# Attention, expert layer and MLP on one core: block means transposed behind the scores, first gated blocks and gate sums moved, operand fetches issued by ScalarE, short output blocks emptied in twos, one output piece moved, start-up loads and filler matmuls rearranged

## The chip, the core and the metric

One core of a Trainium2 chip runs the whole program: TensorE (PE, with its weight loads as PEld), VectorE (DVE), ScalarE (ACT), GpSimd (POOL) and SyncE (SP, which issues the DMAs). The metric is the device time of one launch in microseconds; the median of the runs counts.

## What is computed

```python
def reference(**kwargs):
    attn_out = _attn_ref(q, k, v)              # 2 x 8 heads, 768 tokens, 64 wide
    x = np.ascontiguousarray(attn_out.transpose(0, 2, 1, 3)).reshape(B * S, H * D)
    x = _moe_ref(x=x, **moe_kwargs)            # 1536 x 512, 4 experts of 1024
    return _moe2_ref(x=x, **moe2_kwargs)       # 512 -> 2048 -> 512
...
    k_sum = k.reshape(B, H, nb, block, D).max(axis=3)      # blocks of 32 keys
    v_sum = v.reshape(B, H, nb, block, D).mean(axis=3)
    scores_all = np.concatenate([scores_l_m, scores_s], axis=-1)   # 16-wide band, and 24 blocks
    a = np.exp(scores_all - np.max(scores_all, axis=-1, keepdims=True))
    a = a / (np.sum(a, axis=-1, keepdims=True) + 1e-09)
    return np.matmul(a, np.concatenate([v, v_sum], axis=2))
...
    p = domain_probs / (domain_probs.sum(-1, keepdims=True) + 1e-09)
    for e in range(E):
        out += p[:, e:e + 1] * (np.maximum(x @ w1[e], 0.0) @ w2[e])
...
    h = x @ w_in
    return (h * (1.0 / (1.0 + np.exp(-1.702 * h)))) @ w_out
```

## The kernel before

All matmuls of the two dense layers are done as three products of a high and a low part (hi·hi, hi·lo, lo·hi). A low part is always the original minus the high part, so each operand costs a ScalarE cast and a subtraction on VectorE or GpSimd. The order of the work on every engine is written out by hand: Python closures are called in the order in which the engines get their instructions, and each engine works through its own list in order.

**Attention** runs in 24 groups (batch, pair of heads, four windows of 64 queries) and 27 slots. Slot i (`att_a`, `att_b`) does the scores of group i (PE, then VectorE adds the mask, L239, and takes the maximum), the exponentials on ScalarE (L251), the normalisation of group i-1 on GpSimd (`normalise`, L261), the transposes of group i-2 (L269) and the products with v of group i-3 (`values`, L282). The 24 block means of v come in through `means`: `sums` on VectorE, one PE transpose per pair of heads (L218), a ScalarE scaling (tile `vm`) and, for every group, a GpSimd copy into that group's v tile (`vw` or `v_home`, L220). `values` needs this copy. The weights of expert 0 are split in between (`middle`, L167 and L168). `spin` issues filler matmuls on the identity (L943) in the first slots.

**Expert 0, first tokens** runs between the slots: `early` and `first` compute hidden blocks (L387; PSUM banks 0 to 3 for the first four blocks), `hidden` applies ReLU and gate (`gated`, L331, the VectorE operation that empties the bank) and splits the result (L401, L337), and `second` computes the output blocks into the same banks 0 to 3 (L418). The gates are made by `gates` from the loaded probabilities, written to DRAM (L319) and loaded again spread over all partitions (`load_p`).

**Pairs.** From 150 us on, 44 pairs of hidden tiles follow, each as seven products (L664, PSUM banks 6 and 7, called X and Y) of one step of a Strassen-like scheme. ScalarE copies three of them out of Y (m1, L724; r, L734; q, L739), VectorE adds X to such a copy (L716), then come activation, cast (L711) and low part (L337; on GpSimd for two of the four quarters in a pair whose operands are fetched). Between the products stand pieces of the second layer of the pair before (`fill`): 8 pieces of six matmuls in an expert pair (L782; a main block of 512 tokens in its own bank and a side block of 256 tokens, two side blocks to a bank), 12 pieces of three matmuls in the last layer (L807). `product(y, j, 0)` and `product(x, j, 1)` open a pair. The first piece of a pair uses the high and low parts of both quarters of hidden tile f=1 of the pair before.

The first-layer operands `wA` are computed once and parked in DRAM (`keep`); for 20 pairs they are fetched back (`again`, 1.8 MB into one of two `wA` buffers) by SP. In the pairs in between GpSimd and VectorE also convert the last layer's weights (tile `arena`; SP loads them, L592, and stores them, L631). At the end of the expert layer `of_expert` empties the banks: main blocks and side blocks apart, for each of the four d (L792 and L799 for the side blocks).

```python
        product(y, j, 0, (0, 0), True)
        ...
        nc.scalar.copy(m1, cy)
        lead()
        more()
        product(x, j, 1, (1, 0), True)
        g = total_of(cx, m1)
        ...
        fill(1)
        product(y, j, 4, 1, False)
        nc.scalar.copy(r, cy)
        ...
        fill(3)
        product(y, j, 5, 2, False)
```

## Time and profile before

| | |
|---|---|
| median of 3 runs | 865.87 us (865.20 to 867.35) |
| the profiled execution | 866.81 us, of which the span of the profile is 865.0 us |
| mean granted TensorE clock | 0.993 |
| PE busy | 830.1 us, 96% of the span |
| VectorE, GpSimd, ScalarE busy | 602.0, 479.6, 397.1 us |

The time of an execution is the span and 1.8 us around it. The span has three stages: attention with expert 0 (0 to 150 us), expert pairs (150 to 600 us), pairs of the last layer (600 to 865 us). In the rows further down, an entry in brackets such as "[2.40 <-DMA wA<-kept]" is the idle time of that engine just before the row and what ended it; "x6" is the number of instructions merged into the row.

### The profile page before, as it was taken

The numbers are of one execution on the slowest core, as the hardware profiler recorded it, in microseconds if no ns is written. First come the engines' busy times: TensorE is split into PE (matmuls) and PEld (weight loads), VectorE is DVE, ScalarE is ACT, GpSimd is POOL, SyncE is SP. The second block draws the span as 40 slices with busy tenths as digits, with TensorE's granted clock in tenths as the row PEclk, the third lists the DMA queues.
The fourth block names the chain that finished last, engine by engine and source line by source line (L and its number), as shares of the span: only waits on it lengthen the run. The fifth ranks groups of instructions, "written<-read, shape, count | busy, mean of one in ns | idle before, by whom it ended". The sixth has DMA issues, their size and how long they took to land.

```text
span 865.0 us, 13668 instructions
## 1 busy us (share of the span) xinstructions
PE 830.1 (96%) x5068; PEld 748.7 (87%) x5068; DVE 602.0 (70%) x899; ACT 397.1 (46%) x914; POOL 479.6 (55%) x416
## 2 busy tenths in 40 slices
PE   6978999999999999989999999999899999999998
PEld 5866778899999989889989998999788998998896
DVE  7677538879999884688788688897788753432332
ACT  4766742535444444233333334446556453434442
POOL 6657435656667674265564657867478642323221
PEclk9899999999999999999999999999999999999999
DMA  9853412366767536386776874223534627653422
GB/s 284 255 174 87 138 38 103 117 249 244 266 218 264 207 149 259 114 314 231 277 252 251 287 276 143 77 73 110 183 134 169 232 110 280 207 193 112 150 93 74
DMA packets 48371, 159.93 MB, mean 185 GB/s; under 512 B 5424, under 2 KB 8752, under 8 KB 43184
## 3 DMA queue, kind: packets, MB, share of 16 engines
q1 hardware_dynamic: 48304, 159.06, 53.3%
q8 instruction: 40, 0.66, 0.3%
q14 instruction: 27, 0.22, 0.1%
HBM read 110.78 MB, written 48.26 MB: 184 GB/s over the span
## 4 chain that ended last, share of the span: by engine, by line
PE 72%; DVE 14%; DMA 6%; issue 4%; ACT 2%; POOL 2%; SPq 0%; DVEq 0%; POOLq 0%; ACTq 0%
PE o L782 19%; PE Y L664 17%; PE o L807 13%; PE X L664 5%; PE h L387 3%; DVE S L547 3%; PE o L418 2%; DMA wA<-kept 2%; DVE hid L337 2%; PE sc L231 2%; DVE g L716 2%; PE xo L282 1%; DVE x L452 1%; DMA q<-kq 1%; DVE g L709 1%
## 5 line engine op out<-in xcount | busy, mean ns | idle before, releaser
L782 PE MATMUL o<-hid,wB 128*128 128x512 f32 x1344 | 261.3, 336 | 3.5 <-DVE y L799 2.3
L782 PEld LDWEIGHTS o<-hid,wB 128*128 128x128 f32 x1344 | 214.6, 188 | 25.4 <-DVE y L799 3.0
L576 POOL TENSOR_TENSOR wB<-rawB,wB 128x512 fp32r<-128x512 f32 x88 | 124.9, 1429 | 136.8 <-ACT wB L575 122.0
L807 PE MATMUL o<-wB,hid 128*128 128x512 f32 x576 | 147.8, 393 | 0.0
L711 ACT CAST hid<-g 128x384 fp32r<-128x384 f32 x176 | 90.7, 516 | 117.8 <-DVE g L701 82.4
L337 DVE TENSOR_TENSOR hid<-g,hid 128x384 fp32r<-128x384 f32 (+2 forms) x152 | 129.3, 858 | 19.1 <-ACT hid L711 13.6
L807 PEld LDWEIGHTS o<-wB,hid 128*128 128x128 f32 x576 | 106.9, 188 | 17.0
L552 POOL TENSOR_TENSOR wA<-S,wA 128x512 fp32r<-128x512 f32 x48 | 70.3, 1465 | 45.5 <-ACT wA L551 30.1
L701 DVE SCALAR_TENSOR_TENSOR g<-g,pb 128x384 f32<-128x384 f32 x84 | 83.3, 991 | 2.0
L552 POOL TENSOR_TENSOR wA<-rawA,wA 128x512 fp32r<-128x512 f32 (+1 forms) x48 | 59.7, 1243 | 42.0 <-ACT wA L551 36.4
L664 PE MATMUL Y<-xh,wA 128*128 128x384 f32 x224 | 66.2, 336 | 4.3 <-DMA wA<-kept 2.8
L664 PE MATMUL Y<-xt,wA 128*128 128x384 f32 x336 | 67.5, 335 | 1.7 <-ACT prq L724 1.5
L337 POOL TENSOR_TENSOR hid<-g,hid 128x384 fp32r<-128x384 f32 x40 | 45.6, 1141 | 30.0 <-ACT hid L711 30.0
L724 ACT COPY prq<-Y 128x384 f32<-128x384 f32 x44 | 21.2, 481 | 85.0 <-PE Y L664 68.7
L664 PEld LDWEIGHTS Y<-xt,wA 128*128 128x128 f32 x336 | 56.0, 188 | 4.7 <-ACT prq L724 2.0
L716 DVE TENSOR_TENSOR g<-X,prq 128x384 f32<-128x384 f32 x44 | 24.4, 555 | 43.0 <-PE X L664 40.3
L575 ACT CAST wB<-rawB 128x512 fp32r<-128x512 f32 x88 | 52.5, 619 | 1.4 <-DMA rawB<-wts 1.4
L261 POOL TENSOR_TENSOR s<-s,sm 128x480 f32<-128x480 f32 x24 | 28.3, 1180 | 40.9 <-DVE sm L260 38.5
L708 ACT ACTIVATE sg<-g 128x384 f32<-128x384 f32 x48 | 25.3, 527 | 55.9 <-DVE g L716 55.7
L709 DVE TENSOR_TENSOR g<-g,sg 128x384 f32<-128x384 f32 x48 | 34.2, 713 | 21.5 <-ACT sg L708 19.9
L664 PEld LDWEIGHTS Y<-xh,wA 128*128 128x128 f32 x224 | 41.2, 188 | 7.4 <-DVE arena L605 2.7
L615 POOL TENSOR_SCALAR arena<-arena 128x512 int32<-128x512 int32 x32 | 25.4, 792 | 39.6 <-DVE arena L611 39.6
(451 smaller groups left out, 1633.2 us busy)
## 6 DMA issues: line engine op xcount, KB each, us to landing
kept<-wA SPq DMA_DIRECT2D x20, 1792.0 KB, 6.7
wA<-kept SPq DMA_DIRECT2D x20, 1792.0 KB, 8.7
arena<-w SPq DMA_DIRECT2D x32, 512.0 KB, 4.9
rawB<-wts SPq DMA_DIRECT2D x28, 512.0 KB, 4.0
rawA<-wts SPq DMA_DIRECT2D x16, 512.0 KB, 7.8
w<-arena SPq DMA_DIRECT2D x32, 256.0 KB, 2.5
rawB<-w SPq DMA_DIRECT2D x16, 512.0 KB, 4.3
rawA<-w SPq DMA_DIRECT2D x8, 512.0 KB, 8.0
```

Source lines behind the costliest of these rows:

```text
L261: nc.gpsimd.tensor_tensor(out=s, in0=s, in1=sm.unsqueeze(2).to_broadcast([P, GW, KA]), op=ALU.mult)
L337: engine.tensor_tensor(out=hl, in0=g, in1=hh.bitcast(F32), op=ALU.subtract)
L552: nc.gpsimd.tensor_tensor(out=lo, in0=x, in1=hi.bitcast(F32), op=ALU.subtract)
L575: nc.scalar.copy(hi, rawB[j][:, f])
L576: nc.gpsimd.tensor_tensor(out=lo, in0=rawB[j][:, f], in1=hi.bitcast(F32), op=ALU.subtract)
L664: nc.tensor.matmul(ps[:, 0:HS], ws[w], xs[x][:, k], start=(fresh and k == 0 and m == 0), stop=(k == 1 and m == 2), skip_group_check=True,)
L701: nc.vector.scalar_tensor_tensor(out=g, in0=g, scalar=0.0, in1=pbs[ph, s][:, tok], op0=ALU.max, op1=ALU.mult)
L709: nc.vector.tensor_tensor(out=g, in0=c, in1=sg, op=ALU.mult)
L711: heads.append(lambda: nc.scalar.copy(hh, g))
L716: nc.vector.tensor_tensor(out=g, in0=ps, in1=x, op=ALU.add)
L782: nc.tensor.matmul(o, wB[j][:, w, f, c], tiles[f][:, x, t], start=fr, stop=last, skip_group_check=True,)
L807: nc.tensor.matmul(o, tiles[f][:, x, c], wB[j][:, w, f], start=(new and f == 1 and m == 0), stop=(old and f == 0 and m == 2),)
```

## The change

It has seven parts.

1. `means` is called in `att_a` right after the scores, instead of in `att_b` after the products with v. Its PE transposes (8 in all) go into free columns of the bank that the latest `values` used (bank 7), not into a bank of their own. GpSimd's copy of a slot so stands ahead of its normalisation, split and fold.
2. The gates: the sum over experts becomes two GpSimd additions and a GpSimd add of 1e-9 (`gates_sum`, slot 0), VectorE keeps only the reciprocal, GpSimd multiplies (slot 1 instead of 4); `load_p` moves one slot forward. The probabilities are loaded as SP's 3rd transfer, not its 21st; the q tile of group 4 is the 20th, not the 22nd.
3. `hidden` of blocks 0 to 3 is called about one slot sooner, and its low parts are no longer held back by a queue of their own.
4. The operand fetches `again` are issued by ScalarE, not by SP.
5. The side blocks at the end of an expert stage are emptied two at a time.
6. One second-layer piece (two in the last layer) moves from behind `product(x, j, 1)` to ahead of it; one piece moves from behind `product(y, j, 4)` to ahead of it.
7. `spin` issues 4, 8, 4, 4 filler matmuls in slots 0 to 3 (0, 4, 4, 4 before) and four more behind the transposes of slots 2 and 3. One weight split of slot 3 moves from GpSimd to VectorE. `split_a(0)`, the first pair's operands, is done in eight single steps four and three blocks before the end of expert 0, not in the last three blocks.

```diff
     def means(g):
...
-            ps = bank(5 if b else 4, f"pvs{b}{hp}")
-            nc.tensor.transpose(ps[0:KA, 0:P], vsum[hp % 2], ident)
-            nc.scalar.mul(vms[b, hp][KW:KA], ps[KW:KA, 0:P], 1.0 / BLK)
+            if "ps" not in xo:
+                xo["ps"] = bank(7, "xo")
+            ps = xo["ps"][:, GQ : GQ + P]
+            nc.tensor.transpose(ps[0:KA], vsum[hp % 2], ident)
+            nc.scalar.mul(vms[b, hp][KW:KA], ps[KW:KA], 1.0 / BLK)
...
+    def gates_sum():
+        two, one = ds[:, 0 : NE // 2], ds[:, NE // 2]
+        nc.gpsimd.tensor_tensor(out=two, in0=dp[:, 0 : NE // 2], in1=dp[:, NE // 2 :], op=ALU.add)
+        nc.gpsimd.tensor_tensor(out=one, in0=two[:, 0], in1=two[:, 1], op=ALU.add)
+        nc.gpsimd.tensor_scalar(
+            out=one, in0=one, scalar1=1.0, scalar2=1e-9, op0=ALU.mult, op1=ALU.add
+        )
...
         def again():
             wA[j] = slot("wA", [P, 2, NF - 1, HB], F32R, f"wA{j}", 2)
-            nc.sync.dma_start(out=flat(j), in_=kept[kept_at(j)])
+            nc.scalar.dma_start(out=flat(j), in_=kept[kept_at(j)])
...
         more()
+        fill(1)
         product(x, j, 1, (1, 0), True)
...
-        fill(1)
+        fill(2)
         product(y, j, 4, 1, False)
...
-                    nc.vector.tensor_tensor(
-                        out=y[:, d, 512:S], in0=side, in1=y[:, d, 512:S], op=ALU.add
-                    )
+                    if d % 2:
+                        o = y[:, d - 1 : d + 1, 512:S]
+                        nc.vector.tensor_tensor(out=o, in0=both, in1=o, op=ALU.add)
...
-                    nc.vector.tensor_copy(xf["y1"][:, d, 512:S], side)
+                    if d % 2:
+                        nc.vector.tensor_copy(xf["y1"][:, d - 1 : d + 1, 512:S], both)
...
     def att_a(i):
         if i < NG:
             scores(groups[i])
+        if 2 <= i < NG + 2:
+            means(groups[i - 2])
...
+        spin(SPIN_MORE.get(i, 0))
         if 3 <= i < NG + 3:
             values(groups[i - 3])
-        if 2 <= i < NG + 2:
-            means(groups[i - 2])
...
-        3: [lambda: split(2, A, pool), lambda: split(3, A, dve)],
+        3: [lambda: split(3, A, dve), lambda: split(2, A, dve)],
...
-    SPIN = (0, 4, 4, 4)
+    SPIN = (4, 8, 4, 4)
+    SPIN_MORE = {2: 4, 3: 4}
...
+    for i in range(2):
+        hidden(i)
...
+        if i in (N - 5, N - 4):
+            for _ in range(4):
+                weights.pop(0)()
```

**GpSimd's list in slots 12 and 13.** L220 (L224 after) is the copy of the means into a group's v tile, L261 (L265) the normalisation of a group's score tile s, L168 a weight split, L200 and L181 a fold of k and of v. Before:

```order
L168 TENSOR_TENSOR w0ex_102<-raw_a1_96,w0ex_102 128x512
L220 COPY vw018_659<-vm01_325 24x512
L261 TENSOR_TENSOR s038_860<-s038_860,sm038_893 128x480
L200 COPY kw120_947<-ks12_899 128x4x24
L181 TENSOR_TENSOR vT10_736<-vT10_736 128x24x16
L220 COPY vw028_734<-vm02_398 24x512
L261 TENSOR_TENSOR s100_940<-s100_940,sm100_969 128x480
L200 COPY kw130_1016<-ks13_975 128x4x24
L168 TENSOR_TENSOR w0ex_102<-raw_b_97,w0ex_102 128x512
L181 TENSOR_TENSOR vT11_833<-vT11_833 128x24x16
L220 COPY vw038_831<-vm03_469 24x512
```

The same place in the changed kernel:

```order
L224 COPY vw028_757<-vm02_380 24x512
L265 TENSOR_TENSOR s038_874<-s038_874,sm038_907 128x480
L200 COPY kw120_962<-ks12_913 128x4x24
L181 TENSOR_TENSOR vT10_759<-vT10_759 128x24x16
L224 COPY vw038_845<-vm03_449 24x512
L265 TENSOR_TENSOR s100_954<-s100_954,sm100_983 128x480
L200 COPY kw130_1031<-ks13_989 128x4x24
L168 TENSOR_TENSOR w0ex_102<-raw_b_97,w0ex_102 128x512
L181 TENSOR_TENSOR vT11_847<-vT11_847 128x24x16
```

The copy of group 038 now stands ahead of the normalisation of s100, and so ahead of that slot's fold, split and second fold, which before were all queued in front of it.

**VectorE's list in slots 8 and 9.** g is a hidden block after ReLU and gate, and h2 and h3 are the PSUM banks 2 and 3 that it empties; L239 (L243 after) adds the mask to the scores of a group. Before:

```order
L337 TENSOR_TENSOR hid0_663<-g_664,hid0_663 128x256
L239 SCALAR_TENSOR_TENSOR s018_693<-sc018_684,mask_73 128x480
L244 TENSOR_REDUCE nm018_695<-s018_693 128x4
L259 TENSOR_SCALAR sm008_650<-sm008_650 128x4
L260 RECIPROCAL sm008_650<-sm008_650 128x4
L199 COPY kw038_700<-k03_127 128x4x96
L168 TENSOR_TENSOR w0A1_99<-raw_b_97,w0A1_99 128x512
L337 TENSOR_TENSOR hid0_663<-g_667,hid0_663 128x256
L297 TENSOR_TENSOR xl0_187<-xo024_713,xh0_186 128x256
L187 TENSOR_REDUCE ks10_730<-k10_545 128x24
L331 SCALAR_TENSOR_TENSOR g_741<-h2_373,pb00_480 128x256
L331 SCALAR_TENSOR_TENSOR g_744<-h3_377,pb00_480 128x256
```

The same place in the changed kernel:

```order
L349 TENSOR_TENSOR hid0_625<-g_626,hid0_625 128x256
L349 TENSOR_TENSOR hid0_625<-g_629,hid0_625 128x256
L301 TENSOR_TENSOR xl0_192<-xo014_663,xh0_191 128x256
L343 SCALAR_TENSOR_TENSOR g_687<-h2_399,pb00_430 128x256
L343 SCALAR_TENSOR_TENSOR g_690<-h3_403,pb00_430 128x256
L243 SCALAR_TENSOR_TENSOR s018_715<-sc018_706,mask_73 128x480
L248 TENSOR_REDUCE nm018_717<-s018_715 128x4
```

Banks 2 and 3 are now emptied ahead of the mask of group 018, not behind it, its maxima, a weight split and a fold.

**SP's list of pairs 11 to 14** before, where `kept` is the parked operand tensor in DRAM, `arena1` and `w32` are the last layer's weights in conversion, and the number behind wA is its pair:

```order
L532 DMA wA12_3568<-kept_110 128x3584
L507 DMA rawB12_3688<-wts 128x2x512
L532 DMA wA13_3701<-kept_110 128x3584
L507 DMA rawB13_3777<-wts 128x2x512
L592 DMA arena1_3825<-w64 128x1024 x2
L631 DMA w32_109<-arena1_3825 128x512
L592 DMA arena1_3825<-w64 128x1024
L532 DMA wA14_3907<-kept_110 128x3584
```

ScalarE's list of pair 12 in the changed kernel, where prq is the tile of m1, r and q in turn, and hid a cast of a hidden quarter:

```order
L736 COPY prq12_3695<-Y12_3688 128x384
L723 CAST hid110_3581<-g_3670 128x384
L544 DMA wA13_3717<-kept_111 128x3584
L747 COPY prq12_3695<-Y12_3688 128x384
L723 CAST hid120_3715<-g_3712 128x384
L587 CAST wB12_3733<-rawB12_3698 128x512
L752 COPY prq12_3695<-Y12_3688 128x384
```

The fetch has left SP's list, where it stood behind weight loads and behind stores that wait for GpSimd, and in this pair stands between m1 and r on ScalarE (in pairs 13 to 22 behind q, in the pairs of the last layer ahead of r).

## Rows read from the trace of the kernel before

**Rows 1.** Chain of work that ended last, shares of the span by engine

```profile
PE 72%; DVE 14%; DMA 6%; issue 4%; ACT 2%; POOL 2%; SPq 0%; DVEq 0%; POOLq 0%; ACTq 0%
```

**Rows 2.** Stretches: length, PE, PEld, DVE, ACT, POOL (count), PEclk, DMA share, GB/s

```profile
0.00:25.00 25.00, 16.92 (x151) 14.66 (x152) 16.22 (x33) 12.16 (x42) 17.28 (x31) 0.91 0.97 294
40.00:69.00 29.00, 24.33 (x276) 21.17 (x276) 21.93 (x51) 18.81 (x71) 15.85 (x21) 0.94 0.61 185
69.00:97.00 28.00, 22.85 (x276) 18.54 (x272) 18.34 (x43) 19.34 (x70) 20.07 (x26) 1.00 0.36 110
700.00:850.00 150.00, 150.00 (x746) 134.81 (x745) 52.65 (x95) 62.77 (x131) 45.73 (x39) 1.00 0.45 159
```

**Rows 3.** Waits of PE, 0 to 110: us, times, longest

```profile
PE xo L282 <- POOL vw L220: 5.9, 8, 1.9
```

**Rows 4.** Timeline of PE, start-up: start, length, instruction, [idle before]

```profile
9.21 1.16 PE L943 MATMUL warm<-ident 128*128 128x128 f32 x8
20.72 1.12 PE L282 MATMUL xo<-aT,v_home 120*64 120x64 f32 x16 [2.30 <-POOL v_home L220]
```

**Rows 5.** Short stretches: length, PE busy (count), PEclk, DMA share, GB/s

```profile
24.70:27.40 2.70, 2.70 (x15) 0.53 0.98 347
```

**Rows 6.** Timeline of PE, second products of expert 0

```profile
50.75 3.91 PE L418 MATMUL o<-hid,w0B 128*128 128x256 f32 x18 [2.98 <-DVE g L331]
61.59 3.14 PE L418 MATMUL o<-hid,w0B 128*128 128x256 f32 x24
```

**Rows 7.** Timeline of GpSimd and PE around a late copy of the means

```profile
75.58 0.61 POOL L220 COPY vw<-vm 24x512 f32<-24x512 f32 x1
76.25 0.69 PE L282 MATMUL xo<-aT,vw 120*64 120x64 f32 x16 [1.89 <-POOL vw L220]
```

**Rows 8.** Timeline of PE and VectorE, first products of the first pair

```profile
152.33 0.68 DVE L331 SCALAR_TENSOR_TENSOR g<-h,pb 128x512 f32<-128x512 f32 x1
154.15 1.13 PE L664 MATMUL Y<-xt,wA 128*128 128x384 f32 x5 [1.54 <-ACT prq L724]
```

**Rows 9.** Waits of PE, 130 to 866: us, times, longest

```profile
PE o L782 <- DVE y L799: 2.3, 2, 1.7
PE X L664 <- DVE g L716: 3.2, 5, 1.5
PE o L782 <- DVE acc L792: 1.1, 1, 1.1
```

**Rows 10.** Timeline of PE at starts of fetched pairs

```profile
373.48 0.41 PE L664 MATMUL Y<-xh,wA 128*128 128x384 f32 x1 [2.40 <-DMA wA<-kept]
453.72 0.41 PE L664 MATMUL Y<-xh,wA 128*128 128x384 f32 x1 [1.51 <-DVE arena L605]
```

**Rows 11.** SP's waits of the whole span, and its fetch in pair 13

```profile
SPq L631 <- POOL arena L627: 139.8, 32, 13.6
363.91 0.41 SPq L532 DMA_DIRECT2D wA<-kept  x1
```

**Rows 12.** DMA view of tile wA, 340 to 500

```profile
DMA to landing us min/median/max: 8.2/8.8/10.7
```

**Rows 13.** Timeline of pairs 13, 18 and 23: GpSimd, PE and ScalarE

```profile
356.98 0.52 ACT L711 CAST hid<-g 128x384 fp32r<-128x384 f32 x1
357.40 1.20 PE L782 MATMUL o<-hid,wB 128*128 128x512 f32 x6
359.48 2.24 PE L782 MATMUL o<-hid,wB 128*128 128x512 f32 x12
359.68 0.48 ACT L734 COPY prq<-Y 128x384 f32<-128x384 f32 x1 [1.62 <-PE Y L664]
372.02 1.44 POOL L337 TENSOR_TENSOR hid<-g,hid 128x384 fp32r<-128x384 f32 x1
535.39 1.01 POOL L337 TENSOR_TENSOR hid<-g,hid 128x384 fp32r<-128x384 f32 x1
535.64 0.44 PE L664 MATMUL X<-xh,wA 128*128 128x384 f32 x1 [1.55 <-DVE g L716]
```

More of the change, by code (lines that the diff above doesn't have):

```diff
@@ L211, in sums @@
         )
+    xo = {}
     def means(g):
@@ L278, in values @@
         v = vs.pop(g)
-        ps = bank(7, f"xo{b}{hp}{w0}")
+        ps = xo["ps"] = bank(7, f"xo{b}{hp}{w0}")
         for j in range(GW):
@@ L309, in gates_load @@
         nc.sync.dma_start(out=dp, in_=dpT.rearrange("e (p c) -> p e c", c=NC))
-    def gates():
-        ds = const.tile([P, NC], F32, name="ds")
-        nc.vector.tensor_reduce(out=ds, in_=dp.rearrange("p e c -> p c e"), axis=AX.X, op=ALU.add)
-        nc.vector.tensor_scalar(out=ds, in0=ds, scalar1=1e-9, scalar2=None, op0=ALU.add)
-        nc.vector.reciprocal(out=ds, in_=ds)
-        nc.vector.tensor_tensor(
-            out=dp, in0=dp, in1=ds.unsqueeze(1).to_broadcast([P, NE, NC]), op=ALU.mult
+    ds = const.tile([P, NE // 2 + 1, NC], F32, name="ds")
+    def gates_sum():
[5 more added lines that the diff above has]
+        )
+    def gates():
+        one = ds[:, NE // 2]
+        nc.vector.reciprocal(out=one, in_=one)
+        nc.gpsimd.tensor_tensor(
+            out=dp, in0=dp, in1=one.unsqueeze(1).to_broadcast([P, NE, NC]), op=ALU.mult
         )
@@ L775, in of_expert @@
             n = S - 512
-            main, side = outs["ps"][d], outs["ps"][KC + d // 2][:, d % 2 * n : (d % 2 + 1) * n]
+            main, sides = outs["ps"][d], outs["ps"][KC + d // 2]
+            side = sides[:, d % 2 * n : (d % 2 + 1) * n]
+            both = sides[:, 0 : 2 * n].rearrange("p (d t) -> p d t", t=n)
             for m, (w, x) in enumerate(((0, 0), (0, 1), (1, 0))):
@@ L791, in of_expert @@
                     )
-                    nc.vector.tensor_tensor(
-                        out=y[:, d, 512:S], in0=side, in1=y[:, d, 512:S], op=ALU.add
-                    )
+                    if d % 2:
+                        o = y[:, d - 1 : d + 1, 512:S]
+                        nc.vector.tensor_tensor(out=o, in0=both, in1=o, op=ALU.add)
                 else:
@@ L897, in x_whole @@
         xf[1] = slot("xf", [P, KC, S], F32, "x1")
-    after = {0: [x_parts], 4: [gates], 5: [lambda: load_p(0, 0)], 8: [x_whole]}
+    after = {
+        0: [x_parts, gates_sum], 1: [gates], 4: [lambda: load_p(0, 0)], 8: [x_whole],
+    }
     def later(i, *acts):
@@ L921, in attention_moe_mlp @@
         load_q(groups[hp])
+        if hp == 0:
+            gates_load()
         if hp in (1, 2):
@@ L930, in attention_moe_mlp @@
     load_w(3, A)
+    load_q(groups[4])
     load_vt(0, 3)
     load_v(groups[3])
-    gates_load()
-    load_q(groups[4])
     load_v(groups[4])
@@ L957, in attention_moe_mlp @@
         att_b(i)
-    def hidden_blocks(*blocks):
-        for i in blocks:
-            before = list(pending)
-            pending.clear()
-            hidden(i)
-            for act in before:
-                act()
+    for i in range(2):
+        hidden(i)
     sl = START
@@ L990, in one_slot @@
             sl += 1
+    weights = split_a(0)
     SLOTS = {8: 3}
@@ L996, in attention_moe_mlp @@
         if i == EARLY:
-            hidden_blocks(0, 1)
+            for k in range(2, EARLY):
+                hidden(k)
         first(i)
@@ L1001, in attention_moe_mlp @@
         if i == EARLY:
-            hidden_blocks(2, 3, 4)
+            hidden(i)
         if sl == LAST:
@@ L1016, in attention_moe_mlp @@
             t4 = ops[-1]
-            steps[4:4] = split_a(0)
             load_p(1, 0)
```

## Prediction

> **What bounds the kernel now.** I read the page first, for the chain of work that ended last: 72% of the span is PE, 14% VectorE, 6% DMA [rows 1], so wherever PE is busy without a gap nothing can be won here, since no part of the change removes real matmuls from PE (it adds filler ones). The page has PE busy for 830.1 of 865.0 us, so 34.9 us are left to win at most. Then I read the stretches. In the last layer, 700 to 850, PE is busy in all 150.00 us at full clock [rows 2]: parts 4 and 6 can bring nothing there. In the slots of attention with expert 0 it is busy 24.33 of 29.00 us and 22.85 of 28.00 us [rows 2]. Last I read PE's waits over the two halves of the run, and for each long one the timeline around it, to see which instruction released it and what stood ahead of that instruction on its engine. All terms below are made against the profiled execution, 866.81 us (span 865.0 and 1.81 around it), which lies 0.94 above the median of the runs.
>
> **The change part by part.**
>
> *Start-up (parts 1, 2, 7): −2.0, bounds −3.6 and +1.2.* The first product with v waits 2.30 us for GpSimd's copy of the means [rows 4]. After the change that copy stands ahead of the slot's normalisation, so I count the wait as gone. PE then runs 2.70 us at a granted clock of 0.53 [rows 5], which is the lower of the two levels, 1.2 of 2.4 GHz, after PE had idled; at the full clock it needs 2.70 × 0.53 = 1.43, so 1.27 are to be had if the gap is filled. Both: 3.57. The filler matmuls go from 12 to 28. Four of them are eight instructions and take 1.16 us [rows 4], so sixteen more take 4.6; PE is idle for 25.00 − 16.92 = 8.1 us of the first 25 [rows 2], which covers them as long as they lie in the gaps. If one group of four doesn't, it costs 1.2. The transfer queue is full there (DMA share 0.97 [rows 2]), and the probabilities now go ahead of k of the second pair of heads, which may push later loads back by one issue, some 0.4 us by SP's fetch as the nearest row [rows 11]. I take 2.0, somewhat over half of 3.57, because the loads, not the copy, may set the second slot.
>
> *Slots 8 to 18 (parts 1, 2, 3): −7.6, bounds −3.8 and −11.4.* The idle time is 29.00 − 24.33 = 4.67 and 28.00 − 22.85 = 5.15 [rows 2]. Its named causes are eight waits for the copy of the means, 5.9 us in all, the longest 1.9 [rows 3], and one wait of 2.98 for `gated` (L331) [rows 6]. The copy itself takes 0.61 us and PE starts right behind it [rows 7]; in the order of before the copy has a split and two folds ahead of it in the same slot, and after the change they are behind. So that wait goes, unless the ScalarE scaling of a new pair of heads is late. The 2.98 wait is for banks 2 and 3, which VectorE now empties ahead of a slot's mask, maxima, split and fold. Behind that wait PE had a clock below full: 18 instructions took 3.91 us where 24 of the same take 3.14, so 18 should take 2.36 [rows 6], 1.55 too many. All of it: 4.67 + 5.15 + 1.55 = 11.37. I take two thirds, 7.6, and one third as the lower bound: VectorE is busy 21.93 of the 29 us and GpSimd 20.07 of the 28 [rows 2], so with 11 us less they would be at 85 to 90%, and in an order written by hand some of their lateness comes back as a new wait. What is late next is `normalise` (behind the copy now) and with it the transposes of the next slot.
>
> *First pair (parts 3, 7): −1.4, bounds 0 and −1.54.* The second product into Y waits 1.54 for ScalarE's copy m1 [rows 8]; that copy is queued behind a cast which waits for VectorE's last `gated` block, begun at 152.33 [rows 8]. With `split_a(0)` done a block earlier VectorE has three steps instead of six in the last iteration, so the block comes sooner. If it is PE's own last block that sets it, nothing is won.
>
> *Side blocks (part 5): −3.4, bounds −2 and −3.4.* PE waits 2.3 and 1.1 us to write one half of a bank while VectorE empties the other (L799 and L792) [rows 9]. The two halves are now read once, after both are written. What is late next is the bank's next use, a whole stage away. The emptying of both halves has twice the elements; −2 stands for one of them coming up against a hidden quarter's X.
>
> *The moved piece outside fetched pairs (part 6): −1.3, bounds 0 and −1.7.* Five waits for g, 3.2 us [rows 9], of which 1.55 lie in pair 23 [rows 13] and are counted in the next term. A piece takes 2.24 − 1.20 = 1.04 us [rows 13], and it stands now between the copy m1 and the product that waits. That covers all of the short ones.
>
> *Fetched pairs (parts 4, 6): −1.5, bounds −5.5 and +1.* Two of the pairs with fetched operands begin 2.40 and 1.51 us late [rows 10]. The second is put down to VectorE, which has no part in that product; the first is named right, and both fit the fetch: SP's stores wait for GpSimd 139.8 us in all, the longest 13.6, and in pair 13 the fetch leaves SP only at 363.91 [rows 11] and lands 8.8 us later [rows 12], at 372.7. In the changed kernel ScalarE issues it behind its cast of 356.98 [rows 13], at about 357.5, and it lands by 366.3, far ahead of 371.08, where the pair would begin. So 3.9 us are gained. Against it stands the piece: at the start of a pair it takes the low part of the last hidden quarter, and GpSimd is late with that one. In pair 14 it is wanted at 371.08 + 1.04 + 0.35 (two products of high parts, a third of a piece) = 372.47 and is ready at 372.02 + 1.44 = 373.46 [rows 13]: a wait of 0.99, and the same in pair 19. In pair 24 it is ready at 535.39 + 1.01 = 536.40 and PE is there at 535.64 − 1.55 + 0.35 = 534.44: 1.96 in place of 1.55 [rows 13]. So −3.91 + 0.99 + 0.99 + 0.41 = −1.5. If GpSimd is earlier too, it is −5.5; if the fetch is as late as before, +1. What the fetch itself costs on ScalarE is its issue, 0.41 by SP's row [rows 11], twenty times. It is hidden: ScalarE idled 1.62 us ahead of the copy r [rows 13]. With one piece left between r's product and the next into Y, that is wanted at 359.48 + 1.04 = 360.52, and r ends at 359.68 + 0.48 = 360.16 [rows 13], a slack of 0.36. Beyond that, each late fetch holds PE.
>
> The sum: −2.0 − 7.6 − 1.4 − 3.4 − 1.3 − 1.5 = −17.2, which gives 866.81 − 17.2 = **849.6 us**.
>
> **A rule weighed against a row.** In pair 13 the fetch stands behind a store on SP that waits for GpSimd, and leaves at 363.91 [rows 11], some 6 us behind ScalarE's cast. The Trainium skill, "DMA: Bandwidth & Descriptors", section "Issuing engines are not separate DMA queues", says that transfers started by any engine run on the same 16 DMA engines and that starting them on several engines saves only the small time of the start. By that rule the fetch term is +0.4 instead of −1.5, and the sum 851.5; by the row it is −1.5. I go by the row, since what is saved here is not the start but the queue ahead of it.
>
> **The rivals.**
>
> *B, the slots are bound by VectorE and GpSimd: 855.4, chance 0.19.* Then PE's waits change their names. Start-up brings nothing and slots 8 to 18 half of 7.6: 17.2 − 2.0 − 3.8 = 11.4 are left. For it: the 21.93 of 29 and the 20.07 of 28 us. Against it: ScalarE, VectorE and GpSimd all have gaps there, and the named waits go to a single copy and a single block.
>
> *C, the fetch comes no sooner: 851.5, chance 0.11.* The two late starts stay at 3.9 and cover the low parts' waits; only pair 24's 0.41 is left, so 17.2 − 1.5 − 0.4 = 15.3 is won. For it: the landing takes 8.8 us, which is not issue. Against it: the store that SP waits for.
>
> *D, the fetch holds ScalarE's list: chance 0.10, 874 at the price taken.* ScalarE works in order, and the copies r and q and the casts stand behind the fetch. If it waits there (for its buffer, or for the queue to take it), PE waits for r, twenty times. Each loses what goes beyond 0.36; at a hold of 1.6 us that is 20 × 1.24 = 24.8, so 866.81 − 17.2 + 24.8 = 874.4. It decides from 17.2 / 20 + 0.36 = 1.2 us on. Against it: the buffer was last read by the pair before, which PE has left by then. No ScalarE fetch is in the trace, so a price of 0.4 to 1.6 is open; I take the SP row.
>
> *E, the first pair's own loads set the end of attention: 860.6, chance 0.05.* Then the first three terms, 11.0, are waited away at 150 us. Against it: the DMA share is 0.61 and 0.36 in the slots [rows 2].
>
> **How the numbers follow.** The forecast has 0.55. Its neighbours B and C end on the same side, as does E: faster by over 0.3% (2.6 us, about what this measurement can tell from no change) has 0.90. Of D, holds of 1.1 to 1.35 us per fetch end within 0.3%: 0.04; longer ones slower: 0.06. The range goes from 841, with slots at their upper bound (3.8 more) and fetched pairs at theirs (4.0 more), to 859, which takes in B with another 3.6 of mis-sized terms; what is left out is D, E and the tails.
>
> **What would show it.** Right: no waits of PE for the copy of the means from slot 3 on; the block product that took 3.91 us comes at full clock, and the granted clock from 40 to 69 is 1.00; no waits for L792 and L799 at side blocks; the fetches leave ScalarE some 0.5 us behind a cast and land ahead of the pair; new waits for GpSimd's low part in the pieces that open pairs 14, 19 and 24. Wrong: PE waits for s (L261) or for scores' masks in the slots with the same total (B); the late starts stay (C); idle time of ScalarE behind each fetch, and PE waits for prq (D); a wait for wA at 140 us (E).

## The result, and the profile after

The changed kernel takes 855.62 us (median of 4 runs, 854.52 to 857.45) against 865.54 for the kernel before on the same chip: a ratio of 0.988, with a 95% interval of 0.9857 to 0.9902, so 10 us are won. The profiled execution took 855.0 us, of which the span is 853.2; against the 865.0 of before that is 11.8. Forecast were 849.6 in a range of 841 to 859.

The chain of work that ended last, changed kernel, shares of the span by engine (before: [rows 1]):

```profile
PE 80%; DVE 9%; DMA 4%; POOL 2%; issue 2%; ACT 1%; SPq 0%; DVEq 0%; POOLq 0%; ACTq 0%
```

VectorE's share has fallen from 14% to 9%: the path runs through PE in more of the span. Where that was won and where not is seen in the stretches (columns as in [rows 2]; the last one is pairs 13 to 24 of the changed kernel):

```profile
0.00:25.00 25.00, 18.71 (x186) 16.99 (x187) 18.12 (x35) 12.13 (x43) 17.46 (x34) 1.00 0.96 285
40.00:69.00 29.00, 28.27 (x345) 24.68 (x345) 28.14 (x62) 23.14 (x86) 21.22 (x26) 1.00 0.60 182
69.00:97.00 28.00, 26.83 (x318) 21.78 (x315) 19.47 (x45) 20.48 (x78) 17.90 (x25) 1.00 0.44 125
125.00:150.00 25.00, 22.90 (x100) 19.10 (x99) 16.81 (x18) 8.53 (x15) 10.05 (x6) 0.93 0.27 95
342.90:540.90 198.00, 191.28 (x1083) 176.78 (x1082) 147.45 (x217) 71.42 (x142) 114.08 (x102) 0.99 0.68 231
```

In the slots, 40 to 97, PE's idle time has gone from 9.8 us to 1.9, at full clock, although VectorE is now busy 28.14 of 29.00 us. At the end of attention, 125 to 150, there are 2.1 idle us and a lower clock that the kernel before didn't have. The waits of PE over the whole span (us, times, longest; the longest ones that the text uses) name them:

```profile
PE Y L676 <- ACT prq L747: 2.4, 2, 2.0
PE h L399 <- DVE g L343: 2.1, 1, 2.1
PE Y L676 <- DMA wA<-kept: 2.0, 2, 1.8
PE xo L222 <- DVE xl L301: 1.7, 2, 1.4
PE o L797 <- POOL hid L349: 1.6, 3, 0.7
PE at L273 <- POOL s L265: 1.3, 2, 1.0
PE xo L222 <- DVE vsum L207: 1.2, 1, 1.2
PE o L823 <- ACT y L813: 0.9, 1, 0.9
```

The waits for the copy of the means [rows 3, 4], for the gated block of banks 2 and 3 [rows 6], for m1 in the first pair [rows 8], for the side blocks and, but for 0.2 us, for g [rows 9] are gone. In their place stand a wait for r (L747), one for a gated block at the end of expert 0, late fetches as before, three waits for GpSimd's low part (L349), and in the slots waits for VectorE ahead of the means' transposes (L222).

A clearer book is kept by pairs. The table gives the lead over the profiled execution of before, in us: the start of a pair's first product there less its start here, both from the timelines of PE. Pairs 0, 13, 19 and 25 of before start at 149.65, 355.32, 453.72 and 550.34; the last column is the difference of the spans.

```
                        pair 0  pair 1  pair 12  pair 13  pair 19  pair 25   span
changed                   8.26    9.86    10.81    12.43    13.33     9.45   11.8
f_sp                     10.03   11.62    12.60    14.22    13.36    12.30   14.6
f_act_first               8.59   10.18    11.17    12.79    10.08     0.31    2.7
f_sp_first               10.62   12.20    13.15    14.77     7.50    -0.79    1.6
a_splitback              12.04   12.55    13.50    15.12    16.56    10.44   12.8
best4                    12.82   13.33    14.31    15.93    13.81    11.04   13.4
a_nopiece                10.42   12.20    12.36    13.98    14.57     8.57   11.3
f_low                     8.21    9.79    10.75    12.37    14.35     7.88   10.1
best3                     6.82    8.42     9.40    11.02     8.57     6.90    9.1
a_nospin                  7.99    9.58    10.55    12.17    12.18     6.93    9.3
a_sides                   8.77   10.36    11.33    11.22    12.27     8.02    8.9
a_nomeans                 0.83    2.42     3.40     5.01     5.48     0.88    3.2
b_means                   6.35    6.31     6.32     6.31     4.57     4.78    4.9
```

In the first row the lead grows to 12.4 by pair 13 and falls to 9.5 by pair 25. What is lost there, and the loss between the last block and pair 0, are what the prediction didn't have. The loss from pair 13 to 25 isn't waiting in the main. This is the kernel before in the same pairs (columns as in [rows 2]):

```profile
355.32:550.34 195.02, 188.86 (x1083) 175.36 (x1082) 154.72 (x216) 72.36 (x142) 116.09 (x102) 1.00 0.67 233
```

PE idles 195.02 − 188.86 = 6.2 us there and 198.00 − 191.28 = 6.7 in the changed kernel, so 0.6 of the 3.0 is waiting. The other 2.4 is PE being busy longer with the same products. Of this, 1.7 lies in pair 23, behind the wait for r, where the granted clock was 0.91 (the same pair of before: 15.88 us busy, clock 1.00):

```profile
505.05:524.57 19.52, 17.56 (x93) 16.13 (x92) 15.18 (x21) 7.33 (x15) 12.77 (x11) 0.91 0.48 159
```

### The profile page after: what moved, and what is told of

The parts are those of the page before. It is cut to its first block, busy times and chain, and to the rows that moved or that the text cites. A ratio compares the mean times of both kernels' runs of the same rounds, so it can differ in the third digit from the quotient of the medians.

```text
span 853.2 us, 13743 instructions
## 1 busy us (share of the span) xinstructions
PE 831.1 (97%) x5100; PEld 750.8 (88%) x5100; DVE 582.9 (68%) x893; ACT 393.3 (46%) x914; POOL 477.0 (56%) x419
## 4 chain that ended last, share of the span: by engine, by line
PE 80%; DVE 9%; DMA 4%; POOL 2%; issue 2%; ACT 1%; SPq 0%; DVEq 0%; POOLq 0%; ACTq 0%
PE o L797 21%; PE Y L676 19%; PE o L823 16%; PE X L676 5%; PE h L399 3%; PE o L430 3%; DMA wA<-kept 2%; PE sc L235 2%; DVE hid L349 1%; DVE S L559 1%; PE xo L286 1%; PE at L273 1%; DMA rawB<-wts 1%; POOL wB L588 1%; DVE x L464 1%
## 5 line engine op out<-in xcount | busy, mean ns | idle before, releaser
L797 PE MATMUL o<-hid,wB 128*128 128x512 f32 x1344 | 267.1, 337 | 2.2 <-POOL hid L349 1.6
L797 PEld LDWEIGHTS o<-hid,wB 128*128 128x128 f32 x1344 | 217.0, 189 | 23.4 <-POOL hid L349 2.5
L823 PE MATMUL o<-wB,hid 128*128 128x512 f32 x576 | 150.4, 394 | 0.9 <-ACT y L813 0.9
L349 DVE TENSOR_TENSOR hid<-g,hid 128x384 fp32r<-128x384 f32 (+2 forms) x152 | 111.6, 742 | 17.1 <-ACT hid L723 12.8
L713 DVE SCALAR_TENSOR_TENSOR g<-g,pb 128x384 f32<-128x384 f32 x84 | 87.6, 1043 | 2.0
L349 POOL TENSOR_TENSOR hid<-g,hid 128x384 fp32r<-128x384 f32 x40 | 44.8, 1119 | 27.6 <-ACT hid L723 27.6
L736 ACT COPY prq<-Y 128x384 f32<-128x384 f32 x44 | 21.1, 479 | 81.3 <-PE Y L676 70.2
L747 ACT COPY prq<-Y 128x384 f32<-128x384 f32 x44 | 21.0, 478 | 58.6 <-PE Y L676 58.6
L721 DVE TENSOR_TENSOR g<-g,sg 128x384 f32<-128x384 f32 x48 | 31.9, 664 | 21.6 <-ACT sg L720 19.9
```

Source lines behind the costliest of these rows:

```text
L349: engine.tensor_tensor(out=hl, in0=g, in1=hh.bitcast(F32), op=ALU.subtract)
L713: nc.vector.scalar_tensor_tensor(out=g, in0=g, scalar=0.0, in1=pbs[ph, s][:, tok], op0=ALU.max, op1=ALU.mult)
L721: nc.vector.tensor_tensor(out=g, in0=c, in1=sg, op=ALU.mult)
L797: nc.tensor.matmul(o, wB[j][:, w, f, c], tiles[f][:, x, t], start=fr, stop=last, skip_group_check=True,)
L823: nc.tensor.matmul(o, tiles[f][:, x, c], wB[j][:, w, f], start=(new and f == 1 and m == 0), stop=(old and f == 0 and m == 2),)
```

## Experiments

Names as in the table; "a_" and "f_" are edits of the changed kernel, "b_" of the kernel before.

**The fetch: which queue, and when.** f_sp undoes part 4:

```diff
-            nc.scalar.dma_start(out=flat(j), in_=kept[kept_at(j)])
+            nc.sync.dma_start(out=flat(j), in_=kept[kept_at(j)])
```

> The changed kernel with part 4 undone: SP issues the fetches again, everything else stays. Theory (place): on ScalarE the fetch stands behind the copy q, so it leaves 7.5 us after the start of its pair where SP sent it off after 4.8; this crowds the load of rawB in pair 23 and costs 1.96 there. So without part 4 the waits for the copy r (2.4 us) go, the late starts of the two pairs behind a held store come back (3.9 us instead of 2.0), and the time is within 1.5 us of the changed kernel, 855.6. Rival (hold, case D of the prediction): the fetch holds ScalarE's list in every pair; then it is 2 to 5 us faster than the changed kernel. Rival (case C): the place is of no weight, and waits for wA stay at 2.0 and for r at 2.4.

It took 854.74 us (ratio 0.9875, 0.9847 to 0.9903), the changed kernel's time within the measurement. The waits for r are gone, and those for the late fetches are 5.2 (before: 3.9, [rows 10]), as the place theory has it; a wait of 2.2 for GpSimd's low part stands at the opening of pair 24, where the changed kernel has 0.45. In pairs 13 to 25 it loses 1.9 us where the changed kernel loses 3.0; what that is worth is seen further down.

f_act_first (part 4 kept) and f_sp_first (part 4 undone too) do the fetch as the first of the pair's side steps:

```diff
+        if len(first_acts) == 1:
+            merged.remove(first_acts[0])
+            merged.insert(0, first_acts[0])
         pair(j, merged)
```

> The changed kernel with the fetch as the first of its pair's side steps, so that ScalarE issues it behind the copy m1 and a cast, some 2 us into the pair, ahead of the copy r. Theory (place): it lands some 5 us sooner in every pair, the waits for wA (2.0 us) and for r (2.4 us) go, and the kernel is 3 to 4.5 us faster than the changed one, 851 to 852.6; waits for GpSimd's low part may take 0.5 to 1 of it. Rival (hold): a fetch ahead of r holds r in all 20 pairs, waits for r grow to 5 us and more, slower than the changed kernel. Rival (case C): same as the changed kernel within 1 us.

> The changed kernel with the fetch back on SP, but as the first of its pair's side steps, ahead of that pair's loads and stores. The run with the fetch first on ScalarE lost 12.5 us of its lead in pairs 13 to 25, with waits for GpSimd's low part of 11.6 us. Theory (moment): what counts is when the 1.8 MB move, not which engine sends them off; sent off at the start of the pair they delay the loads of the last layer's weights, the conversion stalls on ScalarE and GpSimd, and the low parts queue behind it. Then this kernel loses as well, 6 to 13 us in pairs 13 to 25, and ends at 859 to 866. Rival (ScalarE's list): the fetch ahead of the copy r was the trouble; then on SP it costs nothing there, the waits for wA go, and it ends at 850 to 853.

f_act_first: 863.89 us (0.9974, 0.9958 to 0.9991); f_sp_first: 864.3 (0.9982, 0.9961 to 1.0003). The first run fits none of its theories: it is 8 us slower than the changed kernel, and the copy r isn't late. It was from this run that the moment theory came, and the second, whose fetch isn't on ScalarE at all, bears it out: from pair 13 to 25 the one loses 12.5 us, the other 15.6. These are the two in those pairs (columns as in [rows 2]):

```profile
342.53:550.03 207.50, 193.98 (x1082) 178.20 (x1081) 145.19 (x217) 71.60 (x142) 116.03 (x102) 0.98 0.63 221
340.55:551.13 210.58, 197.19 (x1083) 181.66 (x1082) 145.48 (x217) 71.61 (x142) 116.22 (x102) 0.96 0.62 220
```

PE idles 13.5 and 13.4 us in them, 7.4 and 7.2 more than in the kernel before, so in waiting the two are alike. The rest of the losses, 5.1 and 8.3, is PE being busy longer, at a mean granted clock of 0.98 and 0.96. First the waits of PE in f_act_first, 300 to 560, then from its view of the tile arena (the last layer's weights in conversion, 355 to 550) for how long an engine sat idle ahead of a conversion step and until what, then a row of its ScalarE:

```profile
PE o L797 <- POOL hid L349: 11.6, 6, 3.5
```

```profile
  DMA arena<-w: 30.8, 10
  ACT arena L614: 16.0, 7
```

```profile
389.15 0.67 ACT L614 ACTIVATE arena<-arena 128x512 f32<-128x512 f32 x1 [4.54 <-DMA arena<-w]
```

The same view of the changed kernel, and of f_sp_first:

```profile
  DMA arena<-w: 13.9, 7
  ACT arena L614: 9.7, 6
```

```profile
  DMA arena<-w: 23.1, 9
```

In pair 18 of f_act_first the way from a late load to PE can be followed: ScalarE's conversion step waits for the load, VectorE's for ScalarE's, and the sum that PE needs stands behind it on VectorE.

```profile
438.46 0.67 ACT L614 ACTIVATE arena<-arena 128x512 f32<-128x512 f32 x1 [4.08 <-DMA arena<-w]
439.16 0.69 DVE L617 SCALAR_TENSOR_TENSOR arena<-arena 128x512 f32<-128x512 f32 x1 [5.50 <-ACT arena L614]
440.37 0.44 PE L676 MATMUL X18b<-xh,wA 128*128 128x384 f32 x1 [1.31 <-DVE g L728]
```

The fetch itself lands in 8.3 us at the median (7.7 in the changed kernel), but the loads of the weights beside it come late: 30.8 and 23.1 us of waiting where the changed kernel has 13.9. ScalarE, VectorE and GpSimd each do the conversion in order with the casts and low parts of the hidden quarters, so PE ends up waiting for a low part, in name GpSimd's; for those waits the way isn't followed row by row here. Which engine starts the fetch matters less than what is in transfer at that moment. The Trainium skill, "DMA: Bandwidth & Descriptors", section "Issuing engines are not separate DMA queues", has all transfers on the same 16 DMA engines whichever engine starts them; the waiting that the early fetch adds, 7.4 us from ScalarE and 7.2 from SP, agrees with it.

**The low parts, and the moved piece.** f_low gives GpSimd other low parts; a_nopiece undoes part 6:

```diff
-            eng = nc.gpsimd if f == n and kept_at(j) is not None else nc.vector
+            eng = nc.gpsimd if f == 0 and kept_at(j) is not None else nc.vector
```

```diff
-        fill(1)
         product(x, j, 1, (1, 0), True)
...
-        fill(2)
+        fill(1)
         product(y, j, 4, 1, False)
```

> The changed kernel with another choice of the two low parts that GpSimd makes in a fetched pair: those of the first hidden tile, not the first and the last quarter on the diagonal, so that none of the tile that opens the next pair is GpSimd's. Theory: the waits for the low part at pair starts (1.6 us) go and nothing takes their place, since GpSimd's second low part is now wanted four pieces later; 1 to 2 us faster than the changed kernel in pairs 13 to 25. Rival: VectorE has no room for the other quarter, and waits for g or for the low part on VectorE come instead, no gain.

> The changed kernel with part 6 undone: the piece stands behind the second product again, not ahead of it. Theory: the waits for GpSimd's low part at the start of a pair (1.6 us, with 0.6 for a weight part behind it) go, the five waits for g come back (3.2 us, of them 1.5 in pair 23 or 24), so the time is 0 to 2 us above the changed kernel's 855.6 and the part is worth about +1 us in all. Rival: the piece is what costs the fetched pairs their lead (3 us from pair 13 to 25); then without it pairs 13 to 25 lose less than 1 us and it is 1 to 2 us faster than the changed kernel.

f_low: 856.43 us (0.9891, 0.9859 to 0.9924), no gain. The waits for GpSimd's low part go, and 3.9 us for r, 3.1 for the fetch and 1.6 for VectorE's low part stand there instead. a_nopiece: 854.35 (0.9868, 0.9836 to 0.9899); its medians can't be told from the changed kernel's. In pairs 13 to 25 it loses 5.4 us, so the moved piece isn't the cause of the loss, which was the rival; between pairs 11 and 12 the piece is worth 0.8 (lead 12.35 at both here, 9.99 to 10.81 in the changed kernel). Its time doesn't show what the part is worth: its profiled execution had the full clock behind the wait for a gated block at the end of expert 0, which the changed kernel's had not (next section), and with it, and 0.5 from the start-up, 2.2 us more lead at pair 0; from pair 1 to the end its lead falls by 0.9, where the changed kernel's grows by 1.9.

**The end of expert 0.** a_splitback puts `split_a(0)` back among the steps of the last blocks:

```diff
-    weights = split_a(0)
...
-        if i in (N - 5, N - 4):
-            for _ in range(4):
-                weights.pop(0)()
...
+            steps[4:4] = split_a(0)
             load_p(1, 0)
```

> The changed kernel with one item of part 7 undone: the first pair's operands (split_a(0)) are again done among the steps of the last blocks of expert 0. Theory (steps packed): in the changed kernel four steps of x stand on VectorE between two gated blocks and hold the one bank, a wait of 2.10 us at 134.2 with a slow clock behind it; undone, that wait and the slow clock go (3.8 us), and the wait of 1.54 for m1 in the first pair comes back, so that the second pair begins some 2 us sooner than in the changed kernel. Rival (density): attention ends 12 us sooner, VectorE is late whatever the order, and a wait of 2 us or more for the gate stays; second pair not sooner, or later.

It took 854.06 us (0.9872, 0.9851 to 0.9893). The wait of 2.10 is gone (one of 0.2 stands at the block before), the one for m1 comes back with 0.8, and pair 1 starts 2.7 us sooner than in the changed kernel. That is as the steps theory has it. In the changed kernel VectorE's rows ahead of the late block, and PE's behind it, are these (the last fence is PE's stretch: length, busy, granted clock, DMA share, GB/s):

```profile
126.92 4.65 DVE L464 TENSOR_TENSOR x<-x 128x768 f32<-128x768 f32 x3
132.59 0.96 DVE L458 TENSOR_TENSOR xt<-x,xt 128x768 fp32r<-128x768 f32 x1 [1.02 <-ACT xt L457]
133.46 0.68 DVE L343 SCALAR_TENSOR_TENSOR g<-h,pb 128x512 f32<-128x512 f32 x1
```

```profile
134.20 0.50 PE L399 MATMUL h<-xh,w0ex 128*128 128x512 f32 x1 [2.10 <-DVE g L343]
```

```profile
134.20:138.60 4.40, 4.40 (x13) 0.63 0.00 0
```

Three differences and a low part that waits for ScalarE stand ahead of the gated block, which alone empties the bank that PE wants at 132.1. Behind the wait the granted clock was 0.63, a part of it at the lower level of 1.2 GHz. Nine of the profiled executions have this wait of 2.10 us: in six the clock behind it was 0.61 to 0.65, in f_sp, f_sp_first and a_nopiece it was 1.00, and these three have 1.3 to 2.6 us more lead at pair 0 than the five others that keep part 1.

best3 deals the x steps out as 5, 3, 3, with the fetch on SP and the low parts of f_low:

```diff
+    STEPS = {3: 5, 2: 3, 1: 3, 0: 0}
...
-            for _ in range(-(-len(steps) // max(rest, 1))):
+            for _ in range(STEPS[rest]):
```

> The changed kernel with three edits: the fetch on SP in its old place, GpSimd's low parts those of the first hidden tile, and the x steps of the last expert 0 blocks dealt out as 5, 3, 3 and not 4, 4, 3. Theory (sum): the wait of 2.10 at the last block shrinks to some 0.6, with full clock behind it, so the second pair begins 1.5 to 3 us sooner than in the changed kernel; the low part waits (2.4 us in the run with the fetch on SP) go, the late wA starts (5 us) stay: 849 to 852. Rival: the low parts on VectorE make it late and the first pair's m1 waits more; 853 to 856.

857.17 us (0.9899, 0.986 to 0.9939): a miss. The wait for the gated block grew to 3.0, and the lead at pair 0 is 6.82. One step fewer ahead of one block was one more ahead of the block before it, and there PE now waits.

**The means and the sooner gates, apart.** b_means is part 1 alone on the kernel before, a_nomeans the changed kernel without it:

```diff
+        if 2 <= i < NG + 2:
+            means(groups[i - 2])
...
             values(groups[i - 3])
-        if 2 <= i < NG + 2:
-            means(groups[i - 2])
```

> The kernel before with part 1 alone: the means behind the scores, their transposes into free columns of the values' bank. Theory: the eight waits for the copy of the means, 5.9 us, and the start-up wait of 2.3 go; the wait of 2.98 for the gated block stays; the last products with v come 5 to 7 us sooner, and the time is 859 to 861. Rival (case B): VectorE and GpSimd bind, the waits change their names (normalised scores, masks), and less than 3 us are won.

> The changed kernel with part 1 undone: the means' copies behind the products with v again, all else as changed. The kernel before with part 1 alone had a lead of 6.35 us at the first pair and kept a wait of 3.7 for the gated block. Theory (two separate causes): the waits for the copy of the means come back, 6 to 8 us, the wait for the gated block stays away; the lead at the first pair falls from 8.3 to 2 to 4 us, and the time is 859 to 862. Rival (VectorE and GpSimd bind, case B): one of the two parts is enough for most of the gain, and the lead at the first pair stays over 6 us.

b_means: 861.51 us (0.994, 0.9919 to 0.9962); a_nomeans: 863.72 (0.9973, 0.996 to 0.9985). PE's waits in the slots, 40 to 110, first of b_means, then of a_nomeans:

```profile
PE o L422 <- DVE g L335: 3.7, 1, 3.7
PE at L273 <- POOL s L265: 1.0, 1, 1.0
```

```profile
PE xo L284 <- POOL vw L222: 6.6, 6, 1.9
```

Part 1 takes away its own wait and leaves the other's, and so do the other parts together (parts 2 and 3 weren't run by themselves). The leads add up: at pair 0 part 1 is worth 6.35 alone and 8.26 − 0.83 = 7.4 on top of the rest, and at the block product ahead of the end of expert 0 the two runs have 6.35 and 4.87, 11.2 in all, where the changed kernel has 12.27. So case B, VectorE and GpSimd as the bound, falls.

**Filler matmuls, side blocks, and the sum.** best4 is f_sp and a_splitback together, with the edits shown there; a_nospin and a_sides have these two:

```diff
-    SPIN = (4, 8, 4, 4)
-    SPIN_MORE = {2: 4, 3: 4}
+    SPIN = (0, 4, 4, 4)
+    SPIN_MORE = {}
```

```diff
-                    if d % 2:
-                        o = y[:, d - 1 : d + 1, 512:S]
-                        nc.vector.tensor_tensor(out=o, in0=both, in1=o, op=ALU.add)
+                    nc.vector.tensor_tensor(
+                        out=y[:, d, 512:S], in0=side, in1=y[:, d, 512:S], op=ALU.add
+                    )
...
-                    if d % 2:
-                        nc.vector.tensor_copy(xf["y1"][:, d - 1 : d + 1, 512:S], both)
+                    nc.vector.tensor_copy(xf["y1"][:, d, 512:S], side)
```

> The changed kernel with the filler matmuls as before (0, 4, 4, 4 and none behind the transposes). Theory: they bring only the clock; without them the first hidden block runs at the lower clock again (granted 0.5 to 0.6 in some 2.7 us), the lead at 40 us falls from 1.7 to 0.4 or less, and the time is 1 to 2 us above the changed kernel's 855.6. Rival: the clock is full anyway because the idle stretch is shorter; the time is the same and the lead at 40 us stays.

> The changed kernel with part 5 undone: each side block is emptied by itself. Theory: the two waits for VectorE's reading of the other half (1.1 in pair 12, 0.6 and 1.7 in pair 28) come back, the wait for ScalarE's copy of y (0.9) goes, and the lead is 2 to 3 us smaller, half of it by pair 13. Rival: with the piece moved the side blocks come at another time and don't wait; no change.

> The changed kernel with two of its items undone, the two that lost time: the fetch back on SP in its old place, and the first pair's operands back among the last blocks' steps. Theory: the leads add up, 12.0 us at the first pair (the run with the operands back), 15 at pair 13, some 2 lost in the fetched pairs as in the run with SP's fetch, 13 at pair 25 and 15.5 at the end: 850 to 851.5, 4 to 5 us faster than the changed kernel. Rival: the fetched pairs' losses depend on how far attention runs ahead of the loads, not on the queue; then 853 to 855.

a_nospin: 857.72 us (0.9907, 0.989 to 0.9924), but not for the reason given: at pair 0 it is 0.27 us behind the changed kernel, and its clock is full where the kernel before had the lower one [rows 5]. The same stretch, 24 to 28, first in a_nospin, then in b_means, which has as many filler matmuls but the old loads (columns as in [rows 5]):

```profile
24.00:28.00 4.00, 3.17 (x41) 1.00 1.05 352
```

```profile
24.00:28.00 4.00, 4.00 (x40) 0.72 1.06 359
```

So the rival's outcome holds: the sixteen further filler matmuls cost nothing and brought next to nothing. Its reason, a shorter idle stretch, isn't borne out: ahead of the first hidden block PE waits 1.24 and 2.31 us in a_nospin, and 2.30 and 0.70 in the kernel before. The clock from 24 to 28 is full in the profiled executions of all twelve kernels with parts 2 and 3, a_nomeans and a_nospin among them, so neither part 1 nor the filler matmuls keep it so; which of the other start-up edits does, no run shows. The other 2 us a_nospin loses in pairs 13 to 25, where its code is the changed kernel's.

a_sides: 857.96 (0.9912, 0.9897 to 0.9927). The waits are back, 1.1 in pair 12 and this one in pair 28, and the lead doesn't grow from pair 12 to 13 (by 1.62 in the changed kernel):

```profile
PE o L797 <- DVE y L814: 2.2, 2, 1.7
```

best4: 854.0 us (0.987, 0.985 to 0.9889), not the 850 to 851.5 that the sum gives. Up to pair 13 the leads do add up, to 15.93; then it loses 4.9 us where f_sp, with the same code there, lost 1.9. First f_sp, then best4, pairs 13 to 24 (columns as in [rows 2]):

```profile
341.10:538.04 196.94, 189.03 (x1082) 175.36 (x1081) 149.70 (x217) 71.94 (x142) 116.22 (x102) 1.00 0.66 233
339.39:539.30 199.91, 192.35 (x1082) 178.27 (x1081) 148.62 (x217) 71.90 (x142) 115.26 (x102) 0.98 0.65 229
```

PE idles 7.9 us in f_sp and 7.6 in best4; what differs is the clock. In pairs 14 and 24, behind waits of 3.1 and 2.2 us, it was 0.90 and 0.91 in best4, and full in f_sp behind waits of 3.6 and 2.2, and these two pairs alone cost best4 3.1 us. So the rival, which puts the loss down to how far attention runs ahead of the loads, isn't borne out either. best4 beats the kernel before by 11.6 us, but not the changed one by more than these runs can tell.

From pair 13 to 25 the changed kernel, a_splitback, a_nospin, a_nomeans and a_sides run the same code, and their profiled executions lose 3.0, 4.7, 5.2, 4.1 and 3.2 us. Here the waits differ too: PE idles 6.7, 9.8, 10.2, 8.9 and 8.7 us. f_sp and best4 lose 1.9 and 4.9. One execution says no more of these pairs than that, so whether ScalarE or SP is the better place for the fetch isn't settled; 12 to 16 us for the early fetch stand far outside it.

## Why the prediction was right, and which terms were not

The range held the time and the sign was right, but two terms had the wrong sign, 8.3 us off together, and a third that was too small made up for 3.0 of it, which is luck. Predicted and measured, in us of time lost (+) or won (−):

| term | predicted | measured | from |
|---|---|---|---|
| start-up | −2.0 | −1.7 | scores at 39.97 before, 38.30 after |
| slots 8 to 18 | −7.6 | −10.6 | the rows below, less the start-up |
| first pair | −1.4 | +2.4 | lead 12.27, and 9.86 at pair 1 |
| side blocks | −3.4 | −3.0 | 1.62 at pair 13; 2.3 [rows 9] to 0.9 |
| moved piece outside fetched pairs | −1.3 | −1.6 | 0.82 at pair 12, 0.8 in the last layer |
| fetched pairs | −1.5 | +3.0 | pairs 13 to 25: 0.6 of waiting, 2.4 of PE being busy longer |

Sum: −11.5, where the spans say −11.8. The rows for the slots are the same block product on PE, the first with `w0ex` over 512 tokens, in the kernel before and in the changed one, 141.49 − 129.22 = 12.27 apart:

```profile
141.49 2.88 PE L418 MATMUL o<-hid,w0ex 128*128 128x512 f32 x12
```

```profile
129.22 2.88 PE L430 MATMUL o<-hid,w0ex 128*128 128x512 f32 x12
```

- **Start-up.** The size was right, the reasons half so. The 2.30 wait went, but PE now waits 1.24 and 1.41 for VectorE ahead of the means' transposes; what is left is the full clock of the first hidden block. The filler matmuls aren't its cause (a_nospin); what is stays open.
- **Slots.** Mechanism right, size too small: I took two thirds of 11.37 because VectorE and GpSimd would be at 85 to 90%. VectorE went to 97% of the first stretch, and PE lost next to nothing by it. The two causes are independent, as the runs with one of them show. 24 matmuls of `second` took 3.13 at once, so the slow clock went too.
- **First pair.** The step that failed is "VectorE has three steps instead of six in the last iteration, so the block comes sooner". For the last block that held: the 1.54 [rows 8] is gone. The block before it got four x steps ahead of it, and PE a wait of 2.10. The slow clock behind that wait was put at nothing. How much it adds varies: f_sp has the same code and the same wait there, kept the full clock, and had 1.8 us more lead at pair 0, 0.1 of it from the start-up.
- **Side blocks.** Right, with one wait that wasn't foreseen: 0.9 for ScalarE's copy of y at the start of the last layer.
- **Moved piece.** Right: but for 0.2 us no product waits for g. The 1.55 [rows 13] belongs to pair 24; the prediction has it under pair 23 at one place.
- **Fetched pairs.** The step that failed is "ScalarE issues it behind its cast of 356.98, at about 357.5". That is the place in pair 12; in pairs 13 to 22 the fetch stands behind the copy q. Rows of ScalarE and PE in pair 14 and 15 of the changed kernel:

```profile
367.72 0.48 ACT L752 COPY prq<-Y 128x384 f32<-128x384 f32 x1 [1.03 <-PE Y L676]
367.72 0.33 ACTq L544 DMA_DIRECT2D wA<-kept  x1
377.81 0.41 PE L676 MATMUL Y<-xh,wA 128*128 128x384 f32 x1 [1.80 <-DMA wA<-kept]
```

The fetch leaves 9.2 us into pair 14, which begins at 358.55, as in pair 19, and 7.5 to 7.9 into the other eight of pairs 13 to 22. SP sent it off 4.3 to 5.4 us into a pair in the eight where no store held it, and after 8.6 and 9.0 in the two where one did, 13 and 18. So in those two it came 1.1 and 1.4 us sooner, and in the rest later. And it crowds others: in pair 23 a weight load took 6.6 us to land (3.9 in f_sp), so ScalarE waits for it and has the copy r late, with the DMA engines busy without a gap (PE's stretches: length, busy, clock, DMA share, GB/s):

```profile
505.00:508.00 3.00, 3.00 (x19) 1.00 0.98 272
508.00:511.00 3.00, 3.00 (x19) 1.00 1.05 376
```

```profile
510.89 1.14 ACT L587 CAST wB<-rawB 128x512 fp32r<-128x512 f32 x2 [3.56 <-DMA rawB<-wts]
513.52 1.75 PE L676 MATMUL Y<-xt,wA 128*128 128x384 f32 x6 [1.96 <-ACT prq L747]
```

The six products behind that wait took 1.75 us where six of the same take 1.20: the clock had fallen, which the prediction's term leaves out. The waits for the low part came where they were forecast, at the openings of pairs 14, 19 and 24, with 0.42, 0.72 and 0.45 in place of 0.99, 0.99 and 0.41 more. Nor would the fetch as early as I had it have won anything: f_act_first has it there, has no late start left, and loses 12.5 all the same.

Of the rivals, B and E don't hold. B's time, 855.4, is the nearest to the one measured, but that is chance: the waits that B says would only change their names are gone, and what is missing was lost at the end of expert 0 and in the fetched pairs. C was nearer than the forecast for the fetch: late starts of 2.0 us stayed. Of D the wait for r came, in two pairs and not in twenty, and not by the fetch's own hold on ScalarE. What stays open is why the same code loses between 3 and 5 us in pairs 13 to 25. The clock behind the waits is one part of it, the waits themselves another; the lead at pair 13 doesn't order the losses, since a_nomeans, with 5.0, loses 4.1 and a_sides, with 11.2, loses 3.2.

## What to carry to other kernels

When a DMA moves to another engine's queue, read from that queue's order, pair by pair, what stands ahead of it, and ask what else is in transfer when it starts: 1.8 MB sent 6 us sooner cost some 9 us more than in its later place (12.5 lost against 3.0), through loads that another engine's list was waiting for and through the lower clock behind PE's waits. Taking steps out of one stretch of an engine's list closes up the rest of it, so look at what now stands right ahead of each instruction that empties a bank. Waits with separate causes added up here even with VectorE at 97%. Read PE's busy time beside its waits: the same products took up to 8.3 us longer, at a lower granted clock, in stretches where the list of waits alone doesn't say so.

## What was not expected of the hardware

After an idle time of PE of 2.10 us at the same place in the same code, the granted clock over the next 4.4 us was 0.63 in the changed kernel and 1.00 in f_sp; over all nine executions with this wait it was 0.61 to 0.65 in six and 1.00 in three. Some 1.7 us of lead hung on it. A longer transfer queue showed itself less in the fetch (landing 7.7 us at the median in the changed kernel, 8.3 in f_act_first) than in the loads started beside it, for which the wait rose from 13.9 to 30.8 us.
